# Block 0's attention by groups of four heads, with a hand-written order of the start

## The chip, the cores and the metric

The kernel runs on one core of a Trainium2 chip. The metric is device time in microseconds (us), the median of several executions. One core has a matrix engine (TensorE, called PE in the profile, with its weight loads shown apart as PEld), VectorE (DVE), ScalarE (ACT), GpSimd (POOL), and SyncE (SP), which here only issues transfers. Each engine works through its own instruction stream and waits on semaphores. Transfers are issued from the SP, ACT and POOL streams and run on 16 shared DMA engines. SBUF is the working memory of 128 partitions, and PSUM is where matmuls write.

## What is computed

A linear attention without softmax is followed by a gated feed-forward network:

```python
# q, k, v: (8 batches, 8 heads, 576 tokens, 64)
kv  = einsum('bhsd,bhse->bhde', k, v)          # 64 x 64 per batch and head
o   = einsum('bhsd,bhde->bhse', q, kv)
o   = o / sqrt(mean(o*o, axis=-1) + 1e-6) * g_norm
x   = o.transpose(0, 2, 1, 3).reshape(4608, 512)
g   = x @ w_gate                               # 512 -> 1536
out = (g * sigmoid(g) * (x @ w_val)) @ w_out   # 1536 -> 512
```

The weights arrive as 8-byte floats and are turned into 4-byte ones on the chip.

## The kernel before

**Blocks.** The 4608 tokens go in nine blocks of 512 (`BLK`). A block holds four tiles of 128 tokens (`T = 4`). Block 0 is made of tokens 0 to 511 of batch 0. From block 1 on, the products of the feed-forward network use a Strassen-like scheme with seven products in place of eight (`L663`, `L826`), for which sums of the weights and activations are made on DVE and POOL. In block 0 the first half of the network is done plainly (`plain_up`, L1492), because its weights are still arriving.

**Who sets the order.** Python traces the instructions in program order. A planner then orders each engine's stream by its own cost estimates, within the data dependencies, and places all semaphores. `tc.issue_after(ins)` puts the instructions traced in its block behind `ins` on the same engine. `in_order()` (L136) chains all instructions traced in its block, per engine, in the order of the program; before the change it is used only in later stages, with one or two engines named. A transfer that is issued from SP or ACT stands in that engine's stream.

**The weights.** `pieces` (L1567) lists 36 pieces: gate and value of hidden group 0, gate and value of group 1, and so on (24 in all, each 512 x 128), then 12 pieces of `w_out`. `load_weights` (L1571) issues their loads on SP; each takes one of the four `ld` buffers. `weights(upto)` (L1579) converts them. One piece takes six instructions (`Words`, L181 to L209): ACT takes the magnitude of the high words (L188), DVE clamps it (L189), DVE extracts the sign bits (L194), DVE joins both (L195), ACT scales the low words (L202), and DVE adds the two (L204). Only then can PE use the piece. For a load, `weights` runs four pieces ahead of the conversion.

**The attention of block 0** is `first()` (L565). The q of 128 tokens and all eight heads is loaded with one token per partition (`load_q`, L350): runs of 256 bytes. It is turned by TensorE against an identity matrix, four transposes per tile of tokens, and copied out of PSUM (`turn_q`, L385). The k and v of 512 tokens come by groups of four heads with four neighbouring tokens per partition, runs of 1 KB; the last 64 tokens of the batch come in four small loads on the ACT queue (`load_first_kv`, L272). `first_kv(g)` (L289) makes the 64 x 64 products of four heads, and ACT and DVE add the two halves. `heads(i)` (L428) multiplies q by them. Before the change `i` numbers the halves of the tokens: half 0 is tiles 0 and 1, for all heads, so that both groups of `kv` must be ready before half 0 begins. `squares` (L442) squares on ACT and sums on DVE. `root` (L452) makes the inverse square root on DVE, by a guess of two and three refinements of three instructions, for both halves at once. `scale` (L483) multiplies by it. `turn_x(i)` (L493) transposes a half's result on TensorE, and ACT copies it out with the gain `g_norm` into `x` (L500). `warm` (L591) issues seven matmuls whose result nobody reads.

**The first hidden groups.** In `alone(0)` (L1648) hidden group 0 is multiplied in two halves of the tokens, each with matmuls of 256 columns (L1501), then groups 1 to 10 with 512 columns: four weight slices for gate and four for value. ACT makes the SiLU (L1506), DVE the product (L1507). Group 11 follows behind the loading of block 1's q. Block 0's result is stored in `store` (L1417).

## Time and profile before

| | |
|---|---|
| median of 3 runs | 1003.6 us (1003.01 to 1003.8) |
| the profiled execution's own time | 1004.81 us |
| its span, first to last instruction | 1003.0 us |
| PE busy | 986.4 us, 98% |
| DVE, POOL, ACT busy | 711.7, 408.7, 231.3 us |
| first transpose on PE | 4.18 us |
| first matmul of k and v | 12.18 us |
| first matmul of hidden group 0 | 30.48 us |
| first matmul of hidden group 2 | 46.24 us in the chain |

The profiled execution lasted 1.8 us longer than its span, which is what lies around it. The page gives shares over the whole span; the start of the kernel fills only its first two slices of 25 us, so it has to be read from the timeline of the engines and from the chain of waits, which follows back from the last instruction what released it.

### The profile page before, as it was taken

How to read it: one execution, taken by the hardware profiler on the slowest of the kernel's cores; microseconds unless marked ns; L12 is line 12 of the kernel's file. 1: busy time of each engine (PE TensorE's matmuls, PEld its weight loads, DVE VectorE, ACT ScalarE, POOL GpSimd, SP SyncE). 2: the span in 40 equal slices, each digit the busy share in tenths (PEclk: the TensorE clock that was granted, in tenths of full speed). 3: DMA queues.
4: the chain of work that ended last, by engine and by line, in shares of the span. 5: the costliest groups of instructions: out<-in, count | busy, mean ns of one | idle time of the engine just before them, and what ended most of it. 6: DMA issues, size and time to landing. Idle time of an engine off the chain costs nothing.

```text
span 1003.0 us, 17761 instructions
## 1 busy us (share of the span) xinstructions
PE 986.4 (98%) x6758; PEld 834.1 (83%) x6758; DVE 711.7 (71%) x1171; ACT 231.3 (23%) x367; POOL 408.7 (41%) x328
## 2 busy tenths in 40 slices
PE   5999999999999999999999999999999999999998
PEld 4544688888888888888888888888888888888998
DVE  2999688678868576656675846666776576666894
ACT  2666111221122312121211211122112112122100
POOL 0000263355544240444566003555651078999300
PEclk9999999999999999999999999999999999999999
DMA  8689742573766855666752365667412556565123
GB/s 220 192 264 272 144 94 110 123 273 94 207 134 132 206 114 167 181 190 167 173 150 43 97 159 150 158 178 179 111 18 68 118 167 206 183 212 160 48 83 97
DMA packets 268261, 151.54 MB, mean 151 GB/s; under 512 B 150288, under 2 KB 250128, under 8 KB 268176
## 3 DMA queue, kind: packets, MB, share of 16 engines
q1 hardware_dynamic: 230928, 144.89, 53.3%
q10 hardware_dynamic: 37184, 5.51, 3.2%
q8 instruction: 54, 0.88, 0.4%
q14 instruction: 31, 0.25, 0.1%
q0 software_dynamic: 64, 0.00, 0.0%
HBM read 109.12 MB, written 32.83 MB: 142 GB/s over the span
## 4 chain that ended last, share of the span: by engine, by line
PE 95%; DMA 2%; ACT 1%; DVE 1%; SPq 0%; POOL 0%; issue 0%; DVEq 0%; POOLq 0%; ACTq 0%
PE b L663 22%; PE b L826 22%; PE c L663 11%; PE c L826 11%; PE a L663 6%; PE a L826 5%; PE b L1501 4%; PE c L1501 4%; PE b L905 4%; PE c L905 2%; PE m L436 1%; PE m L375 1%; DMA arena<-in_v_dram 1%; PE a L905 1%; DMA ld<-in_v_dram 1%; DMA arena<-in_k_dram 0%
## 5 line engine op out<-in xcount | busy, mean ns | idle before, releaser
L826 PE MATMUL b<-arena,t 128*128 128x256 f32 x1008 | 244.5, 381 | 0.0
L826 PEld LDWEIGHTS b<-arena,t 128*128 128x128 f32 x1008 | 190.0, 190 | 29.6 <-DVE r L131 2.4
L131 DVE TENSOR_TENSOR r<-b,r 128x512 f32<-128x512 f32 (+1 forms) x248 | 146.1, 601 | 67.7 <-PE b L826 55.1
L131 POOL TENSOR_TENSOR r<-r 128x256 f32<-128x256 f32 (+1 forms) x90 | 94.7, 1054 | 168.3 <-DMA t<-w 93.3
L131 DVE TENSOR_TENSOR r<-c,r 128x512 f32<-128x512 f32 (+1 forms) x171 | 105.6, 625 | 58.9 <-PE c L826 39.7
L133 POOL TENSOR_TENSOR arena<-r 128x1024 f32<-128x1024 f32 (+1 forms) x54 | 101.8, 1899 | 91.9 <-DVE r L131 48.6
L131 DVE TENSOR_TENSOR r<-a,r 128x512 f32<-128x512 f32 x95 | 60.3, 635 | 100.2 <-PE a L663 64.0
L132 POOL TENSOR_TENSOR t<-wo 128x512 f32<-128x512 f32 x45 | 64.0, 1444 | 164.1 <-DVE wo L131 104.4
L132 DVE TENSOR_TENSOR arena<-arena 128x512 f32<-128x512 f32 (+4 forms) x117 | 121.6, 1055 | 11.3 <-PE b L663 7.0
L826 PE MATMUL c<-arena,t 128*128 128x256 f32 x504 | 122.4, 379 | 0.0
L826 PEld LDWEIGHTS c<-arena,t 128*128 128x128 f32 x504 | 95.7, 190 | 13.2 <-ACT r L840 0.2
L663 PE MATMUL b<-wo,arena 128*128 128x256 f32 x336 | 76.4, 382 | 0.1
L840 ACT COPY r<-b 128x512 f32<-128x512 f32 x54 | 31.6, 585 | 190.1 <-PE b L826 190.1
L663 PE MATMUL b<-t,arena 128*128 128x256 f32 x336 | 74.8, 379 | 0.0
L132 POOL TENSOR_TENSOR t<-arena 128x512 f32<-128x512 f32 x36 | 51.9, 1456 | 54.8 <-PE c L663 21.9
L663 PEld LDWEIGHTS b<-t,arena 128*128 128x128 f32 x336 | 63.8, 190 | 8.7
L663 PEld LDWEIGHTS b<-wo,arena 128*128 128x128 f32 x336 | 63.1, 190 | 9.6 <-DVE arena L133 0.9
L826 PE MATMUL a<-arena,t 128*128 128x256 f32 x252 | 66.1, 379 | 0.0
L826 PEld LDWEIGHTS a<-arena,t 128*128 128x128 f32 x252 | 47.9, 190 | 6.5
L663 PE MATMUL b<-arena 128*128 128x256 f32 x192 | 45.5, 380 | 0.0
L663 PE MATMUL b<-arena,t 128*128 128x256 f32 x192 | 45.4, 379 | 0.0
L1501 PE MATMUL b<-arena 128*128 128x512 f32 (+1 forms) x104 | 43.5, 561 | 0.6 <-ACT arena L500 0.6
(142 smaller groups left out, 1407.5 us busy)
## 6 DMA issues: line engine op xcount, KB each, us to landing
t<-w SPq DMA_DIRECT2D x180, 256.0 KB, 3.3
ld<-in_k_dram SPq DMA_DIRECT2D x26, 288.0 KB, 4.5
ld<-in_v_dram SPq DMA_DIRECT2D x26, 288.0 KB, 5.8
out_dram<-r SPq DMA_DIRECT2D x14, 512.0 KB, 3.2
t<-w SPq DMA_DIRECT2D x54, 128.0 KB, 3.0
ld<-in_moe_w_gate_dram SPq DMA_DIRECT2D x12, 512.0 KB, 4.7
ld<-in_moe_w_val_dram SPq DMA_DIRECT2D x12, 512.0 KB, 4.6
ld<-in_moe_w_out_dram SPq DMA_DIRECT2D x12, 512.0 KB, 4.9
```

Source lines behind the costliest of these rows:

```text
L131: add = lambda e, o, a, b: e.tensor_tensor(out=o, in0=a, in1=b, op=OP.add)
L132: sub = lambda e, o, a, b: e.tensor_tensor(out=o, in0=a, in1=b, op=OP.subtract)
L133: mul = lambda e, o, a, b: e.tensor_tensor(out=o, in0=a, in1=b, op=OP.mult)
L375: self.positions = nc.tensor.matmul(self.kv_ps[r][u * D : (u + 1) * D, g, :], lhsT=k[:, u, c, :], rhs=v[:, u, c, :], start=(c == 0), stop= ...
L436: self.multiplied = nc.tensor.matmul(self.ps[i][u][p : p + D, t, j, :], lhsT=self.qt[rows, tile_t, head, p : p + D], rhs=kvs[b % 3][rows, ...
L663: self.ffn.multiplied = nc.tensor.matmul(ps[:, e], lhsT=lhsT, rhs=rhs, start=first and i == 0 and e == 0, stop=i == self.steps - 1, skip_g ...
L826: self.ffn.multiplied = nc.tensor.matmul(ps[:, i], lhsT=stream.use(self.ffn.n, self.j, o, p), rhs=self.operand(o, p), start=first and i == ...
L840: copied = nc.scalar.copy(out=dst, in_=ps)
L905: self.ffn.multiplied = nc.tensor.matmul(ps[:, i, f], lhsT=self.deep.operand(o, p, c)[:, f], rhs=self.deep.weight(o, p, c, f), start=first ...
L1501: nc.tensor.matmul(t, lhsT=w[f // 2][:, i, P * (f % 2) : P * (f % 2 + 1)], rhs=x[:, i, of], start=(i == 0), stop=(i == NS - 1),)
```

## The change

Block 0 goes by groups of four heads and not by halves of the tokens: `by_heads` is now true for block 0 as well (line 273 of the new kernel), so that `heads(i)` handles four heads for all 512 tokens. q is loaded per group of heads with four neighbouring tokens per partition, as k and v are (`load_first_q`), and each group's q goes ahead of its k and v on the SP queue. The pairs of heads have to be brought side by side before a transpose (`join_q`: two copies per group). The order of tokens in block 0 is then four neighbours per partition, which `store` takes into account. `first()` and the start of `alone(0)` now stand in `in_order()` for all engines. The inverse root of the second group is made by a power of -0.5 on POOL (`inverse`). A SiLU on one column is issued ahead of everything else on ACT. Two pieces of weights are loaded at first instead of four. The contraction over x goes in two parts (`plain_products`): the first two of four slices need only the first group of heads. The products use all 512 columns throughout.

```diff
+    power = consts.tile([P, 4 * NS], F32, name="power")
+    nc.gpsimd.memset(power, -0.5)
+    silu_first = consts.tile([P, 1], F32, name="silu_first")
+    nc.vector.memset(silu_first, 0.0)
+    nc.scalar.activation(out=silu_first, in_=silu_first, func=ACT.Silu)
...
-            self.begun = False
+            self.begun = self.scaled = False
...
-            self.begun = True
+            self.split()
+            return self.join()
...
-        self.by_heads = n == PAIRED
+        self.by_heads = n in (0, PAIRED)
...
             for g in range(2):
-                heads, rows = slice(NS * g, NS * (g + 1)), slice(D * g, D * (g + 1))
+                for x, src in (("k", k), ("v", v)):
+                    nc.scalar.dma_start(
+                        out=last[x][D * g : D * (g + 1)], in_=src[0, heads[g], BLK:S].rearrange("h p d -> p h d")
+                    )
+            for g in range(2):
+                self.load_first_q(g)
                 for x, src in (("k", k), ("v", v)):
                     nc.sync.dma_start(
-                        out=most[x][:, heads], in_=src[0, heads, 0:BLK].rearrange("h (p t) d -> p h (t d)", t=T)
+                        out=most[x][:, heads[g]], in_=src[0, heads[g], 0:BLK].rearrange("h (p t) d -> p h (t d)", t=T)
                     )
...
+        def load_first_q(self, g):
+            to = ld_pool.tile([P, LD], F32, name="ld")[:, 0 : 2 * BLK].rearrange("p (h x) -> p h x", h=NS)
+            heads = slice(NS * g, NS * (g + 1))
+            nc.sync.dma_start(out=to, in_=q[0, heads, 0:BLK].rearrange("h (p t) d -> p h (t d)", t=T))
+            self.q.append(to.rearrange("p (j u) (t d) -> p j u t d", u=2, t=T))
+
+        def join_q(self, g, engines):
+            if g == 0:
+                self.joined = ring().rearrange("p (g j) (t c) -> p g j t c", g=2, t=T)
+            for j, copy in enumerate(engines):
+                to = self.joined[:, g, j].rearrange("p t (u d) -> p u t d", u=2)
+                copy(out=to, in_=self.q[g][:, j])
+
+        def turn_first_q(self, g, engines):
+            if g == 0:
+                self.qt = ring().rearrange("p j (t c) -> p t j c", t=T)
+            for j, (pool, copy) in enumerate(zip((b_psum, c_psum), engines)):
+                ps = pool.tile([P, T, P], F32, name=pool.name[0])
+                for t in range(T):
+                    nc.tensor.transpose(ps[:, t], self.joined[:, g, j, t], ident)
+                copy(out=self.qt[:, :, 2 * g + j], in_=ps)
+
+        def turn_first_x(self, g):
+            for h in range(2):
+                ps = m_psum.tile([P, 2, 2, P], F32, name="m")
+                for e in range(2):
+                    for t in range(2):
+                        nc.tensor.transpose(
+                            ps[:, e, t], self.xts[:, h, t, 2 * g + e].rearrange("p u d -> p (u d)"), ident
+                        )
+                self.copied = nc.scalar.activation(
+                    out=self.x[:, 2 * h + g], in_=ps.rearrange("p e t c -> p e (t c)"), func=ACT.Copy, scale=gain
+                )
...
         def first(self):
-            self.turn_q(0, (b_psum, c_psum))
-            self.first_kv(0, (b_psum, c_psum))
-            last = self.first_kv(1, (b_psum, a_psum))
-            with tc.issue_after(last.ins):
-                self.heads(0, (0, 1), (m_psum, m_psum))
-            with tc.issue_after(self.multiplied.ins):
-                self.heads(0, (2, 3))
-            self.squares(0)
-            with tc.issue_after(self.multiplied.ins):
-                self.turn_q(1, (b_psum, c_psum))
-            with tc.issue_after(self.copied_q.ins), tc.issue_after(self.summed.ins):
-                begun = words[pieces[0]].begin()
-            with tc.issue_after(begun.ins):
-                self.product(1, (b_psum, a_psum))
-            self.warm()
-            self.root(0, 2)
-            self.scale(0)
-            with tc.issue_after(self.squared.ins), tc.issue_after(self.scaled.ins):
+            first, second = words[pieces[0]], words[pieces[1]]
...
+            both = nc.vector.tensor_copy, nc.scalar.copy
+            with in_order():
+                self.join_q(0, both)
+                self.turn_first_q(0, both)
+                self.first_kv(0, (b_psum, c_psum))
+                self.join_q(1, both)
+                self.heads(0, range(2), (m_psum, m_psum))
+                self.square(0)
+                self.sum_squares(0)
+                guess, *refine = self.root_steps(0)
+                guess()
+                refine[0]()
+                self.turn_first_q(1, (nc.scalar.copy, nc.scalar.copy))
+                self.first_kv(1, (b_psum, a_psum))
+                refine[1]()
+                refine[2]()
+                self.scale(0)
+                self.heads(1, range(2), (b_psum, a_psum))
+                first.split()
+                self.square(1)
+                self.turn_first_x(0)
+                self.warm()
+                self.sum_squares(1)
+                self.inverse(1)
+                first.join()
                 weights(1)
+                second.split()
+                second.join()
+                weights(2)
+                self.scale(1)
+            return self.scaled
+
+        def inverse(self, i):
+            z, y = (x[:, i].rearrange("p u t j -> p (u t j)") for x in (self.z, self.y))
+            nc.vector.tensor_scalar(out=z, in0=z, scalar1=1.0 / D, scalar2=eps, op0=OP.mult, op1=OP.add)
+            nc.gpsimd.tensor_tensor(out=y, in0=z, in1=power, op=OP.pow)
...
-            for _ in range(7):
+            for _ in range(3):
...
-            rows = out[BLK * self.n : BLK * (self.n + 1)].rearrange("(t p) d -> p t d", t=T)
+            order = "(t p) d -> p t d" if self.n else "(p t) d -> p t d"
+            rows = out[BLK * self.n : BLK * (self.n + 1)].rearrange(order, t=T)
...
+        def plain_products(self, f, groups, names="gv"):
+            self.ps.setdefault(f, {})
             x = self.att.x[:, 0:4].rearrange("p (h m) i t -> p (m i) h t", h=2)
+            for name in names:
+                w, pool = {"g": (wg, b_psum), "v": (wv, c_psum)}[name]
+                if groups[0] == 0:
+                    self.ps[f][name] = pool.tile([P, 2, HB], F32, name=pool.name[0])
+                for i in range(2 * groups[0], 2 * groups[-1] + 2):
                     nc.tensor.matmul(
+                        self.ps[f][name], lhsT=w[f // 2][:, i, P * (f % 2) : P * (f % 2 + 1)], rhs=x[:, i],
                         start=(i == 0), stop=(i == NS - 1),
                     )
...
+        def plain_h(self, f):
+            h = self.h[:, f].rearrange("p (h t) -> p h t", h=2)
+            self.silus[f] = nc.scalar.activation(out=h, in_=self.ps[f]["g"], func=ACT.Silu)
+            return mul(nc.vector, h, h, self.ps[f]["v"])
...
-    load_weights(4)
-    squared, scaled = blocks[0].first()
+    load_weights(2)
+    scaled = blocks[0].first()
...
+            with in_order():
+                ffn.plain_products(0, (0,))
+                blocks[0].turn_first_x(1)
+                weights(3)
+                ffn.plain_products(1, (0,), "g")
+                ffn.plain_products(0, (1,))
+                weights(4)
+                ffn.plain_products(1, (0,), "v")
+                ffn.plain_products(1, (1,))
+                weights(6)
+                ffn.plain_h(0)
+                weights(8)
+                multiplied = ffn.plain_h(1)
+            for f in range(2, NF - 1):
+                with tc.issue_after(multiplied.ins):
                     weights(2 * (f + 2))
+                ffn.plain_up(f)
```

## The prediction

> **What bounds the kernel now.** First the page: busy times and the slices of 25 us.

> ```profile
> PE 986.4 (98%) x6758; PEld 834.1 (83%) x6758; DVE 711.7 (71%) x1171; ACT 231.3 (23%) x367; POOL 408.7 (41%) x328
> PE   5999999999999999999999999999999999999998
> ```

> TensorE is idle for 1003.0 - 986.4 = 16.6 us in all, and nearly all of it lies in the first slice. The change touches only this start and the stores of block 0, so the question is how much sooner the gapless stretch of PE begins. Second, the chain of waits over the first 50 us (start, length, what):

> ```profile
> 4.99 10.26 DMA arena<-in_v_dram
> ...
> 27.64 1.30 DVE r L133 x2
> ...
> 29.74 0.46 ACT arena L500
> ...
> 32.77 1.28 ACT L1506
> ...
> 35.66 1.99 PE b L1501 x8
> ...
> 46.24 3.43 PE b L1501 x8
> ```

> The start hangs on the load of the second v group (15.25 us), then on DVE's root and scaling, ACT's copy of x and the table load, and only from 35.66 on PE. At 46.24 hidden group 2 begins; from there the chain is PE alone, 6.87 us a group. I take 46.24 as the yardstick: if group 2 begins d earlier and nothing behind it waits, the kernel ends d earlier.

> Third, the timelines of PE and ACT in that stretch, for durations:

> ```profile
> 29.08 1.06 PE L499 MATMUL m<-ident,r 128*128 128x128 f32 x8 [0.26 <-DVE r L133]
> 30.48 1.99 PE L1501 MATMUL b<-arena 128*128 128x256 f32 x8 [0.34 <-ACT arena L500]
> ```

> ```profile
> 29.74 1.26 ACT L500 ACTIVATE arena<-m,gain 128x512 f32<-128x512 f32 x2 [4.33 <-PE m L499]
> 30.90 0.67 ACT L188 ACTIVATE r<-ld 128x512 f32<-128x512 f32 x1
> 32.77 1.28 ACT L1506 ACT_TABLE_LOAD   x1
> ```

> After the two copies of x (29.74), ACT starts the next instruction 1.16 later.

> Fourth, the loads of the first 40 us:

> ```profile
> ld<-in_q_dram SPq DMA_DIRECT2D x4, 256.0 KB, 6.5
> arena<-in_k_dram SPq DMA_DIRECT2D x2, 512.0 KB, 8.8
> arena<-in_v_dram SPq DMA_DIRECT2D x2, 512.0 KB, 9.8
> ```

> Bytes moved, from the same view's rates: 201 and 247 GB/s in the third and fourth microsecond, 177 to 256 up to the seventh, 316 to 336 from the eighth to the twelfth.

> [...] about 200 GB/s while q's 256-byte runs are in, some 325 with k's and v's 1 KB. [...] Here four transposes took 1.08 after the first idle and 0.64 at 29.08; the granted clock shows no change. For the power on POOL no row exists; see below.

> **The change part by part.** Effective DVE pitches in the timeline: 0.60 for a 128x512 of two sources, of PSUM or a reduction; 0.34 for L189 and L194; 0.225 for the small root steps. ACT: 0.57.

> *Loads.* The order is now q, k, v of group 0, then of group 1. First v of before: bytes ahead of it in the queues are q 0.52, k and v 1.05, last tokens 0.26, sum 1.83 MB; 1.83 MB had moved at 9.3, v landed at 12.1, so 2.8 behind. Of the second v: 2.88 MB at 12.6, landed 15.25, 2.65 behind. After, the same bytes stand ahead of the first v, but with q in 1 KB runs: 0.24 MB in the third microsecond, the other 1.57 at 325 GB/s, so 7.85, plus 2.7: K = 10.5. The second v: 1.57 MB more, 4.8 us, 15.4. Its need comes at K + 6.4 = 16.9, so the load goes off the path. The early table load can push the four ACT loads back by 1.3; the last landed at 12.3 before, and the first group's v by 10.9 at latest. They end each pair's sum, so I let them cost nothing; without that cover it is up to 1 us.

> *From K to the scaling, all engines in the written order.* kv(0) takes 2.47 as before (12.14 to ACT's copy at 14.61), copy and add 0.6; heads(0) 1.8 (2.0 and 1.44 before) to K + 4.9; eight transposes 1.5; kv(1) 2.07; copy and add 0.8: K + 9.25. Under it lie the squares, sums and half the root of group 0 and the joining copies (new: four of about 0.6, two of them before K, two beside heads(0)). Then DVE without a gap: six root steps 1.35, scale(0) 1.2: K + 11.8. Clamp and sign of piece 0 0.67, two sums 1.2, one small step 0.22: 13.9. Join and add of piece 0 1.2: 15.1. Piece 1: 0.67 + 1.2: 17.0. scale(1) 1.2: 18.2. The transposes of x for group 0, three warming matmuls (1.3) and its copies (ACT free at 13.8) fit under this.

> *PE from here.* 512 columns cost 0.86 per slice (3.43 for four). Gate, first two slices: 15.2 to 16.9. Value waits for piece 1: 17.05 to 18.8. Transposes of group 1's x: first copy at 19.5. Now the written order bites: ACT does piece 2 only behind both copies, 19.5 + 1.16 = 20.6, done 21.3; DVE, idle since 18.2, needs 0.34 + 0.34 + 0.60 + 0.68: piece 2 is ready at 23.3. PE's next matmul is group 1's gate, which needs piece 2, and the second half of group 0, whose x is there at 20.7, is queued behind it. PE idles from 19.85 to 23.3, 3.45 us. Then 12 slices, 10.3: hidden group 2 begins at K + 33.6 = 44.1.

> *As a sum against before:* the first useful matmul comes at 25.7 and not 30.5 (-4.8); the hole gives 3.45 back; half-width matmuls go (four stretches of 1.84 against two of 3.43, -0.5); small waits of before go (-0.3). Together -2.1, the same as 46.24 - 44.1.

> *What else is removed, at nothing:* the table load of 1.28 (32.77) moves to the start, under the first loads; the SiLU of groups 0 and 1 goes behind six and eight pieces, but PSUM for group 2's value is needed at 47.5 and freed by about 40. The stores have runs twice as long; nothing waits for them.

> *What is late next.* DVE has piece 7 done at K + 33.2 against 45.2, about 1.4 earlier, and after waiting for group 1's product about 1 us ahead of before for the rest of the conversion; pieces stay more than 10 us ahead of PE from group 4 on. Block 1's q loads start when conversion frees a buffer (99.17), so they come 1 us earlier, and their transposes end near 117.1 against a need at 122.49 - 2.1 = 120.4. The sums behind them end near 122.3 (123.3 before); PE needs them at 125.06 - 2.1 = 122.96. Margin 0.7, so nothing is lost.

> *The power on POOL.* It is issued at K + 13.9, and scale(1) begins at 17.0: it is hidden up to 3.1 us. The trace has only additions and the like:

> ```profile
> L132 POOL TENSOR_TENSOR s<-s 128x128 f32<-128x128 f32 x9 | 4.1, 459 | 0.4
> L132 POOL TENSOR_TENSOR s<-s 128x256 f32<-128x256 f32 x5 | 3.7, 732 | 0.0
> ```

> 2.1 ns an element and 0.19 fixed: 0.23 us for 16 elements, the lower bound. [...] Nothing excludes more. I take it as hidden.

> Sum: 1003.0 - 2.1 = 1000.9 span; the profiled run lasted 1.8 more than its span and the median lies 0.6 over it. The difference goes onto the median: **1001.5 us**.

> **Rivals.** About 0.2% (2 us) is what a measurement of this kernel can tell from no change; 1001.6 is the border.

> *The power becomes the bound: slower.* Each microsecond above 3.1 moves scale(1), and with it x, piece 2 and everything behind. It ties with before at 5.2 us and decides above 7.2; at 10 the time is 1008.4. For it: no row of the trace bounds it. [...] 0.13.

> *Loads no sooner: the same.* If the landing lag or the ACT loads keep K at 12.1, group 2 begins at 45.7: 1003.1. For it: equal bytes ahead of the first v. Against: the rate doubles nearly once 1 KB runs prevail. 0.13.

> *Hole smaller or K near 9: faster still.* If piece 2 reaches PE with x (20.7), or the landing lag shrinks with fewer runs outstanding: 2.6 or 1.5 us less, 998.9 to 1000. For it: lag is inferred. Against: the written order. 0.22.

> *The hole cools the clock.* [...] 0.06.

> **How the numbers follow.** The forecast keeps 0.46: 999.9 to 1003.1 by K from 9.0 to 12.0 and some tenths in the pitches; 0.29 of it lies below the border, 0.17 within. Faster: 0.29 + 0.22 = 0.51. Same: 0.17 + 0.13 + 0.06 = 0.36. Slower: 0.13. The range for 8 in 10 is 998.7 to 1004.6: it takes in all but the slow power and the end of the third rival.

> **What would show it.** First matmul of k and v near 10.5 and no wait for the second v; one table load; gate of hidden group 0 near 25.7; a PE hole of some 3.4 us before group 1's gate, ended by DVE's addition of piece 2; hidden group 2 near 44; after it PE without waits. Wrong it is if POOL's power ends after piece 1's addition, if the first k and v product starts after 12, or if PE waits at block 1's transposes.

## The result and the profile after

The time went from 1003.56 us (five executions, 1002.88 to 1003.8) to 1011.8 us (five, 1007.88 to 1013.66). The ratio is 1.0067 with a 95% interval of 1.0053 to 1.0082. The kernel became slower: by 8.2 us between the medians, by 6.7 by the ratio. The forecast was 1001.5 with a range that ended at 1004.6, so it had the wrong sign. The profiled execution of the changed kernel took 1012.32 us, with a span of 1010.5, so 7.5 us more than the span before.

The page of the changed kernel, busy times and slices, looks almost as before:

```profile
PE 987.0 (98%) x6734; PEld 832.2 (82%) x6734; DVE 715.1 (71%) x1173; ACT 231.3 (23%) x369; POOL 412.5 (41%) x330
PE   6899989999999999999999999999999999999998
```

PE's busy time is the same within 0.6 us, its idle time is 1010.5 - 987.0 = 23.5 us and no longer 16.6. PE is now below nine tenths in the second slice, 25 to 51 us, and in the sixth, 126 to 152 us. The loss has two places. The chain of waits of the changed kernel shows the first:

```profile
1.76 7.69 DMA arena<-in_v_dram
...
20.62 1.30 DVE r L133 x2
21.96 1.76 PE m L415 x8
23.72 3.59 PE c L693 x6
27.31 1.72 PE b L1606 x4
...
34.72 0.70 DVE arena L233
35.46 5.40 PE b L1606 x8
40.86 1.73 PE c L1606 x4
42.70 0.69 DVE arena L233
```

The chain before went to PE at 35.66 and stayed there. This one goes from PE to DVE's addition of a weight piece (`L233`), comes back, and at 42.70 goes over to DVE and stays on DVE for the conversion of the weights. PE's own timeline, with the idle time ahead of a row in brackets (the profile counts each 512-column matmul as two records, so x8 are four of them):

```profile
21.96 1.76 PE L415 MATMUL m<-ident,r 128*128 128x128 f32 x8 [1.29 <-DVE r L133]
23.52 3.79 PE L693 MATMUL c<-r,ident 128*128 128x512 f32 x6
27.15 1.88 PE L1606 MATMUL b<-arena 128*128 128x512 f32 x4
...
30.58 1.04 PE L415 MATMUL m<-ident,r 128*128 128x128 f32 x8
35.46 5.40 PE L1606 MATMUL b<-arena 128*128 128x512 f32 x8 [3.84 <-DVE arena L233]
40.70 1.88 PE L1606 MATMUL c<-arena 128*128 128x512 f32 x4
43.45 1.98 PE L1606 MATMUL c<-arena 128*128 128x512 f32 x4 [0.87 <-DVE arena L233]
...
48.70 1.02 PE L1606 MATMUL b<-arena 128*128 128x512 f32 x2
```

The row of hidden group 2 before:

```profile
46.08 3.60 PE L1501 MATMUL b<-arena 128*128 128x512 f32 x8
```

Hidden group 2 begins at 48.70, against 46.08 before. Two things in these rows are new beside the hole of 3.84. Eight records of 512 columns take 5.40 us where eight such took 3.60 before, and the six records of the three warming matmuls take 3.79. The view by stretches, whose last three columns are TensorE's granted clock, the busy share of the DMA engines and GB/s, gives the reason:

```profile
23.00:24.00 1.00, 1.00 (x5) 0.85 (x4) 0.96 (x4) 0.83 (x2) 0.00 (x0) 0.50 0.00 0
...
36.00:37.00 1.00, 1.00 (x3) 0.37 (x2) 0.77 (x2) 0.94 (x2) 0.00 (x0) 0.50 0.92 323
...
38.00:39.00 1.00, 1.00 (x3) 0.48 (x2) 0.00 (x0) 0.00 (x0) 0.00 (x0) 0.50 0.94 321
```

The clock stands at half twice. DVE's timeline shows the other new thing:

```profile
36.11 0.69 DVE L218 SCALAR_TENSOR_TENSOR r<-r 128x512 uint32<-128x512 uint32 x1
42.70 0.69 DVE L233 CUSTOM_DVE_ANT_0 arena<-r 128x1024 uint16<-128x1024 uint16 x1 [5.89 <-ACT r L225]
```

DVE stands still for 5.89 us ahead of the addition of weight piece 3. The view names ACT's scaling, but that began at 36.27 and takes 0.67. What ended at 42.58 is PE's matmul for the value of group 0.

The second place is block 1. First the load of its q on SP's queue and DVE's first transpose of it, before:

```profile
99.17 13.66 SPq L338 DMA_DIRECT2D ld<-in_q_dram  x16
...
115.17 1.25 DVE L391 STREAM_TRANSPOSE r<-ld 128x1024 f32<-128x1024 f32 x1 [6.33 <-DMA ld<-in_q_dram]
```

Then the same rows of the changed kernel, and from the table of waits PE's in the whole execution (total us, times, longest):

```profile
109.42 14.54 SPq L372 DMA_DIRECT2D ld<-in_q_dram  x16
...
126.02 1.25 DVE L463 STREAM_TRANSPOSE r<-ld 128x1024 f32<-128x1024 f32 x1 [7.65 <-DMA ld<-in_q_dram]
```

```profile
PE b L1606 <- DVE arena L233: 3.8, 1, 3.8
PE m L508 <- DVE r L463: 2.7, 2, 1.8
...
PE b L761 <- DVE arena L132: 1.2, 1, 1.2
PE c L1606 <- DVE arena L233: 0.9, 1, 0.9
```

Before, PE had no wait at block 1; its one wait behind 60 us, 0.6 us for a v load, comes at 295 us. Block 1's q loads began at 99.17 before and begin at 109.42 now, because the conversion, which frees the buffers, runs late. PE then waits 2.7 + 1.2 = 3.9 us at block 1. Its first matmul of `w_out`, before and after:

```profile
117.12 5.45 PE L663 MATMUL b<-wo,arena 128*128 128x256 f32 x24
```

```profile
120.15 5.45 PE L761 MATMUL b<-wo,arena 128*128 128x256 f32 x24
```

This is 3.0 later. 3.0 and 3.9 make 6.9 of the 7.5; the other 0.6 I cannot assign.

**Why DVE waits for PE.** The weights of hidden groups 0 and 1 lie side by side in one tile, each with 128 columns of all four slices (`dst = wviews[name][0][j // 2][:, :, P * (j % 2) : P * (j % 2 + 1)]`, `round_w`). The compiled program has for these additions, in DVE's order, with the semaphores each waits for (the pieces' numbers are added here):

```
L233 ISA arena<-r 128x4x256 [waits DVE_49,Activation_49]            piece 0
L233 ISA arena<-r 128x4x256 [waits DVE_49,Activation_49]            piece 1
L233 ISA arena<-r 128x4x256 [waits DVE_49,PE_49,Activation_49]      piece 2
L233 ISA arena<-r 128x4x256 [waits DVE_49,PE_49,Activation_49]      piece 3
L233 ISA arena<-r 128x4x256 [waits DVE_49,Activation_49]            piece 4
```

Pieces 2 and 3 belong to group 1, and they wait for PE, which reads group 0 from the same tile; what piece 3 waits for is the last matmul of group 0's value. No byte is shared. A destination of four stretches with gaps, taken as one range from its first to its last element, covers group 0's columns in the slices between, and that would give this wait. Two experiments below put this to the test.

### The profile page after: what moved, and what is told of

The parts are those of the page before. It is cut to its first block, busy times and chain, and to the rows that moved or that the text cites. A ratio compares the mean times of both kernels' runs of the same rounds, so it can differ in the third digit from the quotient of the medians.

```text
span 1010.5 us, 17722 instructions
## 1 busy us (share of the span) xinstructions
PE 987.0 (98%) x6734; PEld 832.2 (82%) x6734; DVE 715.1 (71%) x1173; ACT 231.3 (23%) x369; POOL 412.5 (41%) x330
## 4 chain that ended last, share of the span: by engine, by line
PE 89%; DVE 7%; DMA 3%; issue 0%; ACT 0%; ACTq 0%; SPq 0%; DVEq 0%
PE b L761 22%; PE b L924 22%; PE c L761 11%; PE c L924 11%; PE a L761 6%; PE a L924 5%; PE b L1003 4%; PE c L1003 2%; DVE r L218 2%; PE m L508 1%; DMA ld<-in_q_dram 1%; DVE arena L233 1%; PE m L447 1%; DVE r L207 1%; DVE r L199 1%; PE a L1003 1%
## 5 line engine op out<-in xcount | busy, mean ns | idle before, releaser
L133 POOL TENSOR_TENSOR arena<-r 128x1024 f32<-128x1024 f32 (+1 forms) x54 | 101.8, 1899 | 87.6 <-DVE r L131 50.3
L132 DVE TENSOR_TENSOR arena<-arena 128x512 f32<-128x512 f32 (+4 forms) x117 | 122.2, 1061 | 10.1 <-PE b L761 7.0
L132 POOL TENSOR_TENSOR t<-wo 128x512 f32<-128x512 f32 x45 | 64.1, 1446 | 149.2 <-DVE wo L131 91.1
L132 POOL TENSOR_TENSOR t<-arena 128x512 f32<-128x512 f32 x36 | 52.4, 1471 | 56.2 <-PE c L761 23.4
L1606 PE MATMUL b<-arena 128*128 128x512 f32 x96 | 45.4, 614 | 4.0 <-DVE arena L233 3.8
## 6 DMA issues: line engine op xcount, KB each, us to landing
t<-w SPq DMA_DIRECT2D x180, 256.0 KB, 3.3
out_dram<-r SPq DMA_DIRECT2D x14, 512.0 KB, 2.9
ld<-in_moe_w_gate_dram SPq DMA_DIRECT2D x12, 512.0 KB, 4.6
ld<-in_moe_w_val_dram SPq DMA_DIRECT2D x12, 512.0 KB, 4.8
ld<-in_moe_w_out_dram SPq DMA_DIRECT2D x12, 512.0 KB, 5.4
```

The costliest lines, as they stand in the source:

```text
L132: sub = lambda e, o, a, b: e.tensor_tensor(out=o, in0=a, in1=b, op=OP.subtract)
L133: mul = lambda e, o, a, b: e.tensor_tensor(out=o, in0=a, in1=b, op=OP.mult)
L1606: nc.tensor.matmul(self.ps[f][name], lhsT=w[f // 2][:, i, P * (f % 2) : P * (f % 2 + 1)], rhs=x[:, i], start=(i == 0), stop=(i == NS - 1),)
```

## Experiments

Every kernel was run in five rounds beside the kernel before, whose medians in the four sets were 1004.03, 1004.34, 1004.49 and 1003.68. Ratios are to it; distances to the change are between medians. Lines are those of each run's own kernel, so the same matmul is L1606, L1608 or L1609.

**1. Group 1's additions slice by slice.** The two additions are each cut into four, one for each slice, so that no destination has gaps.

```diff
-            return nc.vector.tensor_tensor(
-                out=dst.bitcast(U32),
...
+            dst = dst.bitcast(U32)
+            for i in range(a) if apart else ():
+                last = nc.vector.tensor_tensor(out=dst[:, i], in0=mag[:, i], in1=unit[:, i], op=OP.add)
...
+    APART = [(x, j) for x in "gv" for j in (1,)]
```

> The changed kernel, but the last addition of the two weight pieces of hidden group 1 is cut into four, one for each slice of 128 columns; the data and all orders stay. Theory A (the order of DVE's stream is held up because the destination of a group-1 piece, seen as one stretch from its first to its last element, overlaps the group-0 columns that TensorE still reads): the 5.9 us wait of DVE before piece 3's addition is gone, TensorE's 0.9 us wait before group 1's value is gone, piece 7 is done near 47 in place of 52.9, and since block 1's q loads start 5 to 6 us sooner, TensorE's idle time between 125 and 135 (4.0 us) goes to under 1; time near 1005.5, that is 5 to 6 below the changed kernel. Rival B (the wait is a true one, on ACT's scaling or on a transfer): DVE still waits until about 42.7 and the time stays at 1010 to 1012.

Measured: 1006.14 us (1004.99 to 1007.26), ratio 1.002 [1.0012, 1.0028]. The program's additions of pieces 2 and 3 have lost the wait for PE, and DVE's timeline shows both without an idle time ahead of them, four instructions in 0.90 us each:

```profile
33.18 0.90 DVE L237 CUSTOM_DVE_ANT_0 arena<-r 128x256 uint16<-128x256 uint16 x4
...
35.61 0.90 DVE L237 CUSTOM_DVE_ANT_0 arena<-r 128x256 uint16<-128x256 uint16 x4
```

The 5.9 us are gone, and 5.7 of the 8.2 us of loss with them (4.7 of 6.7 by the ratios). So the wait rests on the form of the destination. The hole and the half clock remain: PE's eight records from group 1's gate on start at 33.52 after 3.42 of idling and take 6.65.

**2. The conversion ahead of the second half of group 0.** The additions keep their form, but piece 3 is traced before PE's second half of group 0, as the order before had it.

```diff
+                weights(4)
                 ffn.plain_products(0, (1,))
-                weights(4)
```

> The changed kernel with one line moved: the conversion of piece 3 is traced ahead of the second half of group 0's products in place of behind it, so that TensorE, if anything, has to wait for DVE and not DVE for TensorE. Theory A: the DVE wait of 5.9 us goes, no wait of TensorE takes its place since piece 3 is ready near 37.5 and needed near 40.9; time near 1005.5 as with the cut additions. Rival B: no change, 1010 to 1012. Rival C (the conversion's lateness is made up anyway, and the loss of 4.6 us at block 1 has another cause): DVE's wait goes, but the time falls by less than 1.5 us.

Measured: 1008.57 us (1007.37 to 1008.62), ratio 1.0042 [1.003, 1.0054]: 3.2 better than the change, 3 worse than expected. DVE's wait for PE is gone as expected, so a place in the order makes the wait, together with the form. (The compiled program still ties both additions to PE, and that of the kernel before ties piece 2's, but to reads of group 0 that are done by then.) Why it gains less than experiment 1 isn't shown. PE's eight records after the hole took 6.67 us in place of 5.40, but so they did in experiment 1 (6.65, with a granted clock of 0.50 in each microsecond from 33 to 39). What differs in its trace is block 1: the planner put DVE's first reduction ahead of the sums that PE needs, and DVE waited there 4.4 us for ACT's squares (1.2 in experiment 1), PE behind it 0.9; experiment 7 finds no price of that order.

**3. Piece 2 split and joined ahead of the transposes of group 1's x.** The forecast's hole came from ACT taking piece 2 only behind its two copies of x.

```diff
                 ffn.plain_products(0, (0,))
+                third = words[pieces[2]]
+                third.split()
+                third.join()
                 blocks[0].turn_first_x(1)
```

> The changed kernel with the first four instructions of piece 2's conversion (magnitude, clamp, sign, join) traced ahead of the transposes and copies of the second group's x. Theory A: piece 2 is ready near 31.3, TensorE's hole of 3.8 us before group 1's gate shrinks to under 0.5, the clock stays at full rate from 35 to 40, group 1's value then waits about 0.8 for piece 3, whose addition still waits for TensorE but until 37 only; hidden group 2 begins near 43 to 44, time near 1002.5. Rival B (the hole is the transposes' own latency): the hole stays above 2.5 us and the time above 1008.

Measured: 1007.63 us (1006.23 to 1010.22), ratio 1.0037 [1.0025, 1.0049]. It misses what it was made for: `join` does not include ACT's scaling of the low words, which stays behind the copies and ended the wait. The hole was 2.19 us and not 0, and the eight records after it took 5.40 again, as at the change's clock of 0.50.

**4. The hole filled.** Three matmuls whose result nobody reads are put ahead of group 1's gate.

```diff
                 weights(3)
+                ps = a_psum.tile([P, 2, HB], F32, name="a")
+                for _ in range(3):
+                    nc.tensor.matmul(ps, lhsT=ident, rhs=blocks[0].x[:, 0], start=True, stop=True)
```

> The changed kernel with three more matmuls whose result nobody reads, in the hole of TensorE behind the transposes of the second group's x; it computes the same. Theory A (the clock falls to half because TensorE stands idle there): the granted clock stays at 1.0 from 35 to 40, the eight matmuls of group 1's gate and group 0's gate take 3.4 us in place of 5.4, DVE's wait for TensorE ends 2 us sooner, and the time falls by 2 to 4 us, to about 1008. Rival B (the clock's fall has nothing to do with the hole): 5.4 us again, time unchanged.

Measured: 1007.99 us (1006.72 to 1008.34), ratio 1.0036 [1.0024, 1.0048], so 3.8 better than the change with more work. In its profile the granted clock was 1.00 in each microsecond from 34 to 40 and the eight records took 3.70:

```profile
30.59 2.74 PE L1764 MATMUL a<-arena,ident 128*128 128x512 f32 x6
34.61 3.70 PE L1606 MATMUL b<-arena 128*128 128x512 f32 x8 [1.28 <-DVE arena L233]
```

**5. Piece 2 wholly ahead.** As the third, with the scaling.

```diff
                 third.join()
+                third.scale()
```

> The changed kernel with the first five of piece 2's six conversion instructions, ACT's scaling among them, traced ahead of the transposes and copies of the second group's x; only DVE's addition stays behind. Theory A (the hole in TensorE is ACT's order: both of piece 2's ACT instructions stand behind the copies of x): piece 2 is ready near 31, the hole of 3.8 us goes, the clock stays full; group 1's value still waits about 1 us for piece 3; hidden group 2 near 43 to 44 in place of 48.7; time 1004 to 1006, with the remaining loss at block 1. Rival B: the hole stays, since TensorE waits for something else, and the time stays near 1008.

Measured: 1004.4 us (1002.86 to 1009.38), ratio 1.0005 [0.9994, 1.0016]. The hole is gone, and with it 7.4 us of loss (6.2 by the ratios), though DVE's wait for PE at piece 3 is still there:

```profile
31.27 1.04 PE L415 MATMUL m<-ident,r 128*128 128x128 f32 x8
32.17 3.70 PE L1606 MATMUL b<-arena 128*128 128x512 f32 x8
...
38.46 1.98 PE L1606 MATMUL c<-arena 128*128 128x512 f32 x4 [0.87 <-DVE arena L233]
```

A PE that isn't held up ends group 0 sooner, so the wait for it shrinks too: piece 3 was added at 37.71 after 2.45 us of idling, where the change had 42.70 and 5.89. The two faults feed each other, and that is why experiments 1 and 5 win 5.7 and 7.4 of only 8.2 (by the ratios 4.7 and 6.2 of 6.7).

**6. Slices and piece 2 together.**

> Both edits of before together: the additions of group 1's pieces cut into four, and piece 2's conversion ahead of the copies of x. Theory A (the two waits are all that stood against the predicted start): TensorE works without a hole from the first gate product on, hidden group 2 begins near 42 (46.24 in the kernel before), and what remains lost is about 1 us at block 1; time 999.5 to 1001.5. Rival B (something else at block 1 takes the gain back): hidden group 2 near 42, but the time above 1003.

Measured: 1002.84 us (1000.28 to 1007.01, 21 executions), ratio 0.9989 [0.9982, 0.9997]. The start is as the forecast had wanted it and better: hidden group 2 begins at 40.58 and the first matmul of `w_out` at 111.94, 5.2 sooner than before. The profiled execution, with 1000.48 one of the fastest, keeps 4.3 of that in its span; the median is only 1.5 lower.

**7. The sums of block 1 in their old place.** On top of experiment 6, block 1's reductions are held behind the second sum of hidden values, as in the order before.

```diff
-                    fill[p]()
+                    with tc.issue_after(self.second.ins) if self.n == 0 and p == 1 else ExitStack():
+                        fill[p]()
...
-                two()
+                ffn.second = two()
```

> The same with one more constraint: the squares and scalings of block 1's attention are put behind the second sum of block 0's hidden values on DVE, as they stood in the kernel before. Theory A (in the changed kernel the planner put block 1's first reduction ahead of that sum, so DVE waits there for TensorE and TensorE then for DVE): the wait of TensorE at block 1's second product goes, 0.9 to 1.8 us less than without; 998.5 to 1000.5. Rival B (the planner's order costs nothing): same as without.

Measured: 1003.02 us (1001.22 to 1006.29), ratio 0.9985 [0.9979, 0.9992]: no difference from experiment 6. That order isn't what eats the gain. Here the first matmul of `w_out` is at 112.94 in the profile, 4.2 sooner than before, and the span of 1001.2 only 1.8 shorter.

**8. The early table load alone.** The kernel before, with the one-column SiLU at its start and nothing else.

```diff
+    silu_first = consts.tile([P, 1], F32, name="silu_first")
+    nc.vector.memset(silu_first, 0.0)
+    nc.scalar.activation(out=silu_first, in_=silu_first, func=ACT.Silu)
```

> The kernel before with one part of the change alone: a SiLU on one column ahead of everything else on ACT, so that the table load of 1.28 us at 32.77 moves to the start. It stood in the chain of waits there: between 0.5 and 1.3 us faster, 1002.3 to 1003.1, if what follows it was not waiting for piece 2's addition anyway (34.8); if it was, within 0.4 of the kernel before.

Measured: 1004.22 us (1002.95 to 1005.48), ratio 1.0 [0.9992, 1.0008]. Its profiled execution began hidden group 2 at 44.12 and took 1003.3 us, that of the kernel before 46.08 and 1004.81. But 1.36 of these 1.96 us stand already at the first product of k and v (10.82 and 12.18), which waited for v's load, and the medians do not differ. So I take most of it for a difference between executions. It also warns of single profiles: in the change's order this product began between 9.18 and 10.51 in twelve of them, so sooner than in both profiles of the old order, but by anything from 0.3 to 3.0 us.

**9. A warming matmul earlier.** On top of experiment 7: one of the three goes ahead of the transposes of group 0's x, into the time in which PE waits for DVE's scaling.

```diff
+                self.warm(1)
                 self.turn_first_x(0)
-                self.warm()
+                self.warm(2)
...
```

> Kernel: the one of the run before with slices, the early piece 2 and block 1's sums in their old place; in addition one of the three warming matmuls stands ahead of the transposes of group 0's x instead of behind them. All computed. In its base's executions the mean granted clock was 0.998 or less in 14 of 21 (median of these 1003.1 us) and 0.999 or 1.0 in the others (median about 1002.4; those at 1.0 about 1001.8), and its profile had the clock at 0.5 from 22 to 25.3 us. Theory A (TensorE has too little work from 20.2 to 21.7, and whether that halves the clock is left to chance): the mean clock is 0.999 or above in most executions, the six warming records take 2.7 us in all, the gate of group 0 begins at 25.2, the median falls by about 1 to 1002.0. Rival B (the halving comes from something else, as the start after the first idle): clocks and times spread as before, 1003.0.

Measured: 1002.9 us (1001.28 to 1005.88), ratio 0.9984 [0.9977, 0.9991]. Half of it came: 15 of 17 executions had a mean clock of 0.999 or 1.0, against 10 of 21 in experiment 7 (the expectation counts those at 0.999 on the wrong side), and in the profile the warming records took 1.12 and 1.88 us, with a granted clock of 1.00 from 20 to 27 us. One stretch at half clock, of 3.4 us as in the change (22.2 to 25.6 us), is 1.7 of 1003, or 0.0017 of the mean, so the mean tells whether it occurred. But the median did not fall. In the profile the first matmul of `w_out` is at 112.32, 4.8 sooner than before, and the span of 1002.3 is 0.7 shorter: PE waits 2.9 us at block 1, and 0.7 for a v load later.

**10. No warming.** Experiment 7 without the three matmuls.

> Kernel: the same base, without the three warming matmuls (nothing reads what they compute). Theory A (low activity of TensorE halves the clock): without them it is idle from 22.7 to 25.2 as well, the clock halves in most executions and the gate and value of group 0 take up to 3.4 us each instead of 1.9: 1003.5 to 1005. Rival B (the warming is only work in the way of the gate, 1.7 us too much where the clock is halved): the gate begins at 25.2 in every execution: 1001.5 to 1002.

Measured: 1004.86 us (1001.4 to 1007.64), ratio 1.0 [0.999, 1.001], 1.8 worse than with them (1.5 by the ratios). All 14 executions had a mean clock of 0.998 or less, and in the profile the gate of group 0 took 3.28 us where experiment 9 has 1.98, with a granted clock of 0.66 between 26 and 27 us:

```profile
25.77 3.28 PE L1609 MATMUL b<-arena 128*128 128x512 f32 x4 [2.40 <-DVE arena L238]
```

**11. The root on DVE.** Experiment 7 with the old guess and refinements for group 1 in place of the power on POOL.

```diff
-                self.inverse(1)
+                self.root(1)
```

> Kernel: the same base, group 1's inverse root by DVE's three refining steps instead of the one power on POOL; all computed. Theory A (the power of 3.24 us on POOL is hidden under DVE's work on pieces 0 and 1): the steps, about ten small ones of 0.2 us by the trace of after, go onto DVE's chain, pieces 0 and 1 or the scaling come 2 us later, and the time is 0.5 to 2 us longer, 1003.5 to 1005. Rival B (POOL's power holds the scaling, or slows DVE while it runs): the time falls, 1002 or less.

Measured: 1004.74 us (1002.72 to 1006.93), ratio 1.0003 [0.9995, 1.0011], 1.7 worse. The gate of group 0 begins at 27.82 in its profile, after 2.12 us of waiting for DVE's addition. So POOL's power is a gain, and it doesn't hold the scaling.

**12. Block 1's q in half as many transfers.** On top of experiment 9. Block 1 takes 64 tokens of each head from the batch before in transfers of 8 KB and the others in transfers of 56 KB; here it takes all of them from one batch in transfers of 64 KB. So 64 tokens of each head are other ones than the computation asks for, while bytes and work stay the same.

```diff
+            if self.n == 1:
+                spans = [(self.n, 0, 0, BLK // 32)]
```

> Kernel: the one with a warming matmul moved ahead; in addition block 1's q is loaded in 16 transfers of 64 KB in place of 32, half of them of 56 and half of 8 KB (the same bytes; 64 tokens per head are then taken from the wrong place, which is a changed computation at an unchanged amount of work). In the base's profile these loads occupy SP's queue from 100.0 to 115.5 and the first transpose of block 1's q on DVE waits 8.2 us for them, to 117.19; PE then waits 3.6 us in all at block 1. Theory A (what start the edits win is lost at block 1 because its q comes no sooner, and the count of transfers sets when it comes): the first transpose starts 3 us or more earlier, PE's waits at block 1 fall under 1 us, and the median falls from 1002.9 to 1000 to 1001.3. Rival B (the bytes and their 128-byte runs set it, not the count): the transpose starts as before, 1002.5 to 1003. Rival C (q comes sooner but nothing of block 1 depends on it): earlier transpose, 1002.9.

Measured: 999.64 us (999.25 to 1000.28), ratio 0.9958 [0.9944, 0.9972]. First the load on SP's queue and DVE's first transpose of block 1's q in experiment 9, then in this one:

```profile
100.03 15.47 SPq L374 DMA_DIRECT2D ld<-in_q_dram  x16
...
117.19 1.25 DVE L465 STREAM_TRANSPOSE r<-ld 128x1024 f32<-128x1024 f32 x1 [8.22 <-DMA ld<-in_q_dram]
```

```profile
100.42 8.36 SPq L376 DMA_DIRECT2D ld<-in_q_dram  x8
...
111.36 1.25 DVE L467 STREAM_TRANSPOSE r<-ld 128x1024 f32<-128x1024 f32 x1 [2.19 <-DMA ld<-in_q_dram]
```

With the same bytes in half as many transfers the row lasts about half as long (0.97 and 1.05 us a transfer). Much of that is waiting: issuing one took 0.45 us, the median of the 224 q transfers on this queue in the trace before, and in the one after. In the compiled program each of these transfers waits for a semaphore which the transfer eight places before it, four on its own queue, raises when it has landed. An estimate from that and from the landing time of 2.2 us before: sixteen transfers, four at a time, 8.8 us; before, ACT's queue took 8.89 for its sixteen, which start later than SP's:

```profile
104.71 8.89 ACTq L338 DMA_DIRECT2D ld<-in_q_dram  x16
```

q comes 5.8 us sooner, PE waits for nothing from 40 us to the end, and the time falls by 3.3 (2.6 by the two ratios). Of the 5.0 that the first matmul of `w_out` is sooner than before (112.10), the span of 997.5 keeps all. That is what held experiments 6, 7 and 9: their PE came to block 1 sooner, and block 1's q did not. The profiles agree: in those of experiments 12, 6, 10, 7, 9 and 11 the first transpose of q began at 111.36, 114.44, 114.75, 116.75, 117.19 and 119.00, and the spans stand in the same order, 997.5, 998.7, 999.6, 1001.2, 1002.3 and 1002.8.

## Why the prediction was wrong

**What held.** K, the start of the first product of k and v, was forecast at 10.5 and came at 9.59, towards the third rival's 9; nothing waited for the second v. There is one table load, at 1.59, of 1.28 us. POOL's power took 3.24 us, 14 times the lower bound of 0.23 that I had from POOL's additions, and above the 3.1 for which it was said to be hidden; nothing in the trace before bounded it from above. It ended at 27.37 and the scaling of group 1 began at 27.88, because DVE took 4.0 us (from 23.88) for pieces 0 and 1. So that it was hidden is luck; in experiments 1, 2 and 4 there were 0.18 us to spare. The hole before group 1's gate was forecast at 3.45 and measured at 3.84, and DVE's addition of piece 2 ended it. The rival with the slow power did not occur.

**What was mis-sized.** The gate of group 0 began at 27.15. From the measured K the forecast's K + 15.2 gives 24.8. Of the 2.35 between, about 1.0 is DVE's: piece 0 was there at 25.73 and not at K + 15.1 = 24.7. The other 1.4 is PE's own lateness. I put the three warming matmuls at 1.3 us, against my own 0.86 for 512 columns, which gives 2.6; they took 2.74 at full clock in experiment 1, and there still ended as piece 0 came. Here they took 3.79, and the transposes ahead of them 1.76 in place of 1.09, because the clock was at half. The rival in which the hole cools the clock, given 0.06, happened; the trace before, at 1.00 from 20 to 118 us, shows no such fall. Eight records took 5.40 where I had 3.43: 2.0 us. The halving from 22 us on (0.50 from 22.2 to 25.6 in the change) occurs in the profile of the change and of experiments 5 and 7 and not in those of 1, 4 and 6, where the clock was 1.00 in each microsecond from 18 to 27, with the same work on PE up to there; what decides it isn't shown. The forecast also read that the granted clock shows no change in the first idle. The clock's records begin only at 19.86 us in the trace before and at 18.80 in the one after, so the view's 1.00 ahead of that is no measurement: four transposes took 1.08 and 1.12 us at 4.18 and 6.63, and 0.66 at 20.58.

**The step that failed.** It is "What is late next", in the clause that DVE is "about 1 us ahead of before for the rest of the conversion" and that pieces stay ahead of PE. DVE stood 5.89 us ahead of piece 3. I had followed the written order for what each engine does next, but not for what a write must wait for: in the new order the addition of group 1's pieces comes after PE's reads of group 0 in the same tile, and the program ties the two together. Experiments 1 and 2 show that this wait needs both the gaps in the destination and the new order. That the planner compares the whole range of a destination with gaps is the reading that fits both; how it does so isn't shown. Piece 7 was done at 52.90, where the forecast had K + 33.2 = 43.7 and the kernel before 45.20. By the sums of `w_out` the lag behind before is 10.7 us (114.34 against 103.63); how 7.7 grew to that stays open. It moved block 1's q loads by 10.25, and gave 3.9 us of waits at block 1.

From the forecast 44.1 for hidden group 2 to the measured 48.70 it adds up: gate 27.15 for 25.7, 1.45; hole 0.4; clock 2.0; the wait of 0.87 for piece 3: 4.7 of 4.6.

**A second step that would have failed.** The yardstick was that group 2 earlier by d ends the kernel earlier by d, with a "margin 0.7, so nothing is lost". Even a start without the faults does not carry through. In the profiles of experiments 7 and 9 the first matmul of `w_out` came 4.2 and 4.8 sooner, and 1.8 and 0.7 arrived at the end. The margin was taken from q transposes that "end near 117.1" and move with the conversion. But the first of them waits 6.33 us for q's load in the profile before, and SP's half of that load lasts 11.9 to 15.5 us from one profile to another, sixteen of 32 small transfers on two queues; what makes it vary isn't shown. Experiment 12 shows that this is where the gain went. The size of one of these transfers counted for little: in the trace before, 8 KB landed 2.2 us after their issue and 56 KB after 2.2 to 2.3.

## What to carry to other kernels

When an order is written by hand, ask of each write not only what it needs but who still reads the tile that it goes into, and whether the tracking of dependencies sees a write with gaps as one range; one engine stuck on such a wait, as DVE here for 5.89 us, holds everything queued behind it. A gain at the start is worth only what the next fixed arrival leaves of it (1.8 of 4.2 us and 0.7 of 4.8 in experiments 7 and 9), so look for the next transfer that some engine already waits for in the profile before. Where many small transfers wait for each other's landing, count them: here sixteen lasted 15.47 us on SP's queue, and eight with the same bytes 8.36 (experiments 9 and 12). Put spare work of TensorE where it is idle (experiment 4 filled a hole, and the eight records behind it took 3.70 us in place of 5.40), and not where it stands in the way of work that is about to be ready (in the change the warming matmuls took 3.79 us, and the gate of group 0 began 1.4 after its weights were there).

## What the runs showed of the hardware

- The granted clock was 0.50 behind holes of PE of 3.84 us (the change, from 35.9 to 39.3 us, so for 3.4) and of 3.42 (experiment 1, in each microsecond from 33 to 39, and 0.75 in the next). Eight records of 512 columns took 5.40 and 6.65 us there in place of 3.60. They took 6.67 and 5.40 behind holes of 3.85 and 2.19 (experiments 2 and 3), and four took 3.28 and 3.61 in place of 1.88 behind 2.40 and 2.12 (experiments 10 and 11); the mean clocks of these four profiles were 0.997 and 0.998. With three filling matmuls ahead of a remaining hole of 1.28 the clock was 1.00 (experiment 4). It was also 0.50 in the three microseconds from 23 to 26 (experiment 5), from 22 to 25 (experiment 7) and from 22.2 to 25.6 us (the change), behind a wait of only 1.29 us that followed matmuls of 64 columns, so a long hole is not needed; behind the same wait it was 1.00 in experiments 1, 4 and 6.
- A power of 128 x 16 values of 4 bytes took 3.24 us on POOL, 1.6 ns a value or 203 ns for each of the 16 columns. An addition of 128 x 128 took 0.46 us there.
- In the profile before, block 1's q transfers of 8 KB landed 2.2 us after their issue and those of 56 KB after 2.2 to 2.3. Sixteen such on SP's queue, each waiting for the landing of the one four before it, lasted 0.97 us a transfer (experiment 9), eight of 64 KB 1.05 (experiment 12). The executions of experiment 12 (five) lie within 1.0 us, those of experiment 9 (17) within 4.6; that the edit narrows them isn't shown by so few.
